# First four row tiles turned as centred rows, their loads on two queues, and a new order of the work

## The chip, the cores and the metric

The kernel runs on one core of a Trainium2 chip. A core has five engines with their own instruction streams: TensorE (PE) for matmuls and transposes through a matmul, VectorE (DVE), ScalarE (ACT), GpSimd (POOL) and SyncE (SP). TensorE writes only to PSUM, in banks; the other engines copy results from there to SBUF. Transfers between HBM and SBUF, and transposes during a transfer, are issued by an engine's queue (here SP, POOL and, in few places, ACT) and carried out by 16 DMA engines.

The metric is the device time of one execution in microseconds, as the median of several runs. A profiled execution gives in addition a trace of every instruction and transfer. Its span runs from the first to the last instruction; the time of the same execution is a little longer than its span.

## The reference

With x of 2048 rows and 512 columns (bf16), LN a layernorm over a row without weights, and xn = LN(x), the result is `x + s * g`:

- **s**: q, k, v = xn @ wqkv, in 32 heads of 16 columns. Row t attends to the eight rows t, t-2, ..., t-14 (rows below 0 are masked), with a softmax over the eight logits; the weighted sum of v is multiplied by wo.
- **g**: `silu(B(xn))`. Within B, `h = gelu(LN(xn) @ w1)`; the four column groups of h are shifted by -1, +1, -2 and +2 rows and multiplied by w2; that is added to xn and gives x1; then `x1 + gelu(LN(x1) @ w3) @ w4`, with 1376 hidden columns.

A layernorm of xn is again a scaling of the centred row: with variance var of a row of x, LN(LN(x)) is (x - mean) times 1/sqrt(var * (1 + eps) + eps * eps).

## The kernel before

The 2048 rows are handled as 16 tiles i of 128 rows, four to a chunk c of 512 rows. Tile i of a chunk holds every fourth row of it, so that a partition reads whole stretches of x. Each operation is a small function ("step") with tile numbers and, for matmuls, the PSUM bank as arguments. One long string, `ORDER`, lists all steps in the order in which they are issued; `ev.2` is the step `ev` for tile 2 and `qk.0.3.2` is q/k column block 3 of chunk 0 into bank 2. The string was made by a planner outside of the kernel. Each engine and each queue works through its own steps in that order, and semaphores hold a step until its operands and its buffer are ready. So a step that waits holds up all that stands behind it on the same engine or queue.

The steps that this case turns on, with their lines:

- `ldxp`, `ldxc` load x by pairs of tiles or by chunks; `ldv`, `ldw1`, `ldqk` (L227 to L241) load the halves of the weights. All go through SP's queue.
- `warmup` (L318) runs matmuls on zeros before there is data.
- `st` (L332) computes mean and variance of a tile on VectorE; `sq0` (L337) the square root of the variance on ScalarE, for tiles 0 to 3; `nm0` (L343) the reciprocal and the normalised tile xr, on VectorE.
- `tr0` (L353) turns a normalised tile of the first chunk on TensorE; `ev0h` and `ev0a` (L359, L363) copy it from PSUM into `xnT`, on ScalarE, in halves or whole.
- From chunk 1 on, `nmv` (VectorE) or `nm` (ScalarE) normalises a tile, and `xT` (L422) turns two tiles with a DMA transpose on SP's queue.
- `v`, `w1` and `qk` (L467, L492, L440) are four matmuls each of 128 x 128 by 512. `v` and `w1` need one turned tile, `qk` all four of its chunk.
- `ev` (L479) copies v out of PSUM and `sv` stores it to HBM; `eh` (L504) applies the gelu to w1's result with a row factor; `eqk` copies q and k.
- `rp`, `rs`, `rr` (L371, L384, L391) compute the row factors: a sum on VectorE, a power on GpSimd, products on VectorE. For tiles 0 to 3, `rr` multiplies the factor by the square root of `sq0`, since the tile that goes into `w1` is normalised already.
- Later come `pw` (products q * k, VectorE), `lg` (their sums over a head, TensorE), the softmax, `vp` (products with v, VectorE) and `ws` (their sum, TensorE), `w2`, `w3`, `w4` and `wo` with `xa`, `ya` and `sg`, which take their results from PSUM on VectorE, and the stores.

In `ORDER` before, the start on TensorE is: warm-up, `tr0` of tiles 0 and 1, `v.0`, `v.1`, `w1.0`, `tr0.2`, `w1.1`, `tr0.3`, then `v` and `w1` of the rest and the eight `qk` of chunk 0.

Of the kernel before, what the change touches and what calls it, by code (L numbers as in the profile page):

```python
# [8 lines left out]
AF = mybir.ActivationFunctionType  # L9
ALU = mybir.AluOpType  # L10
# [12 lines left out]
qk.0.4.1 qk.0.5.5 nmv.6 nmv.7 st.11 ldxc.s.3 st.10 st.8 eqk.0.3 eqk.0.5 qk.0.2.2 eqk.0.0  # L23
qk.0.6.4 eqk.0.2 st.9 eqk.0.4 qk.0.7.3 eqk.0.6 eqk.0.7 pw.0.1 rp.5 st.15 st.13 rp.4 xT.3 hTr.0
ldw2.s hTr.1 w1.4.1 v.5.4 ldwo.s.0 ev.5 w1.5.3 v.4.2 ev.4 qk.1.4.4 rs.4 sv.4 v.6.5 w1.7.2 rr.3
rr.2 eh.4 pw.0.2 kh.1 ev.6 sv.5 rs.5 nb.4 pw.0.0 st.12 eqk.1.4 eh.5 w1.6.1 qk.1.1.4 qk.1.2.3
v.7.5 hTr.2 nm.8 nm.9 w2.1.0 pw.0.3 nb.5 rp.6 eh.6 xT.4 vl.s.1.1 eh.7 st.14 rp.7 lg.0.0 rs.7
eqk.1.2 lg.0.1 ev.7 pw.0.5 w2.0.5 rs.6 eqk.1.1 nm.11 nm.10 pw.0.4 sv.7 qk.1.5.4 sv.6 xT.5
# [45 lines left out]
def kernel(  # L74
# [131 lines left out]
    qs = {"s": nc.sync, "a": nc.scalar, "g": nc.gpsimd}  # L206

    @step
    def ldxc(q, c):
        x_c[c] = rot("xc", c, 2, [P, TPC, D])  # L210
        qs[q].dma_start(
            out=x_c[c],
            in_=x2[c * CH : (c + 1) * CH, :].rearrange("(p i) d -> p i d", i=TPC),
        )
# [69 lines left out]
        nc.gpsimd.memset(mhalf[:], -0.5)  # L284

    @step
    def c_zero():
        nc.gpsimd.dma_start(out=v_dram[0:PADK, :], in_=warm[0:PADK, :])
        nc.gpsimd.memset(hT[:, :, :, 0:HALO], 0.0)
        nc.gpsimd.memset(hT[:, :, :, HALO + S // TPC :], 0.0)  # L290

# [47 lines left out]
            ve1[:, i // 2, i % 2 : i % 2 + 1], mv1[:, i, 1:2], AF.Sqrt, bias=eps_t[:]  # L339
        )  # L340

    @step
    def nm0(i):  # L343
        nc.vector.reciprocal(out=rstd1(i), in_=ve1[:, i // 2, i % 2 : i % 2 + 1])
        nc.vector.tensor_scalar(
            out=xr[i], in0=xtile(i), scalar1=mv1[:, i, 0:1], scalar2=rstd1(i),
            op0=ALU.subtract, op1=ALU.mult,
        )

    tr_t = {}  # L350

    @step
    def tr0(i, b):  # L353
        tr_t[i] = bank(b, (P, ND, P), BF16)
        for dt in range(ND):
            nc.tensor.transpose(tr_t[i][:, dt, :], xr[i][:, dt * P : (dt + 1) * P], ident[:])

    @step
    def ev0a(i):  # L359
        nc.scalar.activation(xnT_tile(0)[:, i, :, :], tr_t.pop(i), AF.Copy)  # L360

    @step
    def ev0h(i, h):  # L363
        nc.scalar.activation(
            xnT_tile(0)[:, i, 2 * h : 2 * h + 2, :], tr_t[i][:, 2 * h : 2 * h + 2, :], AF.Copy
        )
        if h:
            del tr_t[i]
# [121 lines left out]

    @step
    def w1(i, b):  # L492
        c, jj = i // TPC, i % TPC
        pt = mm["w1", i] = bank(b)
        for dt in range(ND):
            nc.tensor.matmul(  # L496
                pt, lhsT=xnT[c][:, jj, dt, :], rhs=w1_sb[:, dt, :],
                start=(dt == 0), stop=(dt == ND - 1),
            )

# [374 lines left out]
```

## Time and profile before

| | us |
|---|---|
| median of 3 runs (189.77 to 190.12) | 189.9 |
| the profiled execution | 190.75 |
| its span | 189.0 |
| PE busy | 182.8 (97%) |
| VectorE busy | 165.1 (87%) |
| ScalarE busy | 112.8 (60%) |
| GpSimd busy | 42.7 (23%) |
| mean DMA rate over the span | 208 GB/s |

The profile is one execution. Busy times are sums over instructions; those of matmuls include the time in which one runs behind another, so PE's is rather too high. "Idle before" an instruction is put down to whatever released it last. The chain of waits follows the work back from the last instruction, at each step to what it waited for. In a tile's answer, "DMA to landing" is the time from issue until the last of the 16 DMA engines has reported. In the windows, each engine has its busy share of the stretch, and the last columns are the granted TensorE clock, the DMA share and GB/s.

### The profile page before, as it was taken

What the parts mean: (1) busy time and instruction counts of PE and PEld (TensorE: products, weight loads), DVE (VectorE), ACT (ScalarE), POOL (GpSimd) and SP (SyncE); (2) the same over time, 40 slices, a digit from 0 to 9 for tenths busy, and PEclk for the clock granted to TensorE, in tenths of its full rate; (3) what the DMA queues carried; (4) which work ended last, traced back from release to release, by engine and by line L of the source; (5) the groups of instructions that cost most, each with busy time, mean ns of one, the idle gap of its engine ahead of it and who ended that gap; (6) DMA issues with size and microseconds to landing.
All of it is one profiled execution on the core that took longest, in us unless ns stands there. A gap on an engine that the chain in (4) does not pass through costs nothing.

```text
span 189.0 us, 3685 instructions
## 1 busy us (share of the span) xinstructions
PE 182.8 (97%) x1430; PEld 87.0 (46%) x1430; DVE 165.1 (87%) x270; ACT 112.8 (60%) x189; POOL 42.7 (23%) x70
## 2 busy tenths in 40 slices
PE   7999999999999999999999999999999999999990
PEld 2444445445444545444444555444455444444450
DVE  2694797997999899999989998999999999989554
ACT  3578669666595636045941465969529664742780
POOL 4157156423010702010450000000050003005350
PEclk9999999999999999999999999999999999999998
DMA  5994986987969929965989929999974999796783
GB/s 164 315 352 115 199 248 141 194 238 137 233 120 286 278 64 224 222 87 190 399 162 361 274 57 134 254 401 277 189 190 95 254 335 238 210 254 106 88 106 116
DMA packets 47842, 39.25 MB, mean 208 GB/s; under 512 B 35251, under 2 KB 41889, under 8 KB 47777
## 3 DMA queue, kind: packets, MB, share of 16 engines
q1 hardware_dynamic: 45008, 35.14, 74.6%
q0 software_dynamic: 2528, 3.69, 10.9%
q8 instruction: 11, 0.18, 0.4%
q10 hardware_dynamic: 288, 0.20, 0.3%
q14 instruction: 7, 0.05, 0.1%
HBM read 26.41 MB, written 5.78 MB: 170 GB/s over the span
## 4 chain that ended last, share of the span: by engine, by line
PE 85%; DMA 4%; DVE 4%; issue 2%; POOL 2%; SPq 1%; ACT 1%; POOLq 0%
PE mm L668 20%; PE mm L685 18%; PE mm L443 15%; PE mm L611 8%; PE mm L496 7%; PE mm L471 6%; PE lg L543 4%; PE mm L768 4%; DMA xc<-in_A_x_dram 3%; PE mm L729 3%; POOL out_dram L835 2%; DMA out_dram<-xr 1%; DVE st L333 1%; DVE xr L775 1%; DVE xr L786 1%
## 5 line engine op out<-in xcount | busy, mean ns | idle before, releaser
L530 DVE TENSOR_TENSOR pw<-qT,kT 128x2048 bf16<-128x2048 bf16 x32 | 38.3, 1214 | 3.4 <-PE lg L543 2.4
L668 PE MATMUL mm<-x1T,w_sb 128*128 128x512 bf16 (+1 forms) x176 | 40.9, 379 | 0.0
L685 PE MATMUL mm<-w_sb,h 128*128 128x512 bf16 (+1 forms) x176 | 39.4, 379 | 0.0
L677 ACT ACTIVATE h<-mm 128x512 bf16<-128x512 f32 (+1 forms) x44 | 23.9, 602 | 23.3 <-PE mm L668 17.6
L716 DVE TENSOR_TENSOR vs<-vs,att 128x4096 bf16<-128x4096 bf16 x16 | 36.2, 2285 | 0.0
L443 PE MATMUL mm<-xnT,wqk_sb 128*128 128x512 bf16 x128 | 30.6, 379 | 0.0
L835 POOL DMA_DIRECT2D out_dram<-xr x12 | 11.0, 1117 | 74.0 <-DVE xr L775 74.0
L668 PEld LDWEIGHTS <-w_sb 128*128 128x128 bf16 (+1 forms) x176 | 17.6, 100 | 20.4
L685 PEld LDWEIGHTS <-h 128*128 128x128 bf16 (+1 forms) x176 | 16.9, 98 | 20.8 <-issue 0.4
L443 PEld LDWEIGHTS <-wqk_sb 128*128 128x128 bf16 x128 | 12.4, 98 | 15.0
L452 ACT ACTIVATE kT<-mm 128x512 bf16<-128x512 f32 x16 | 9.4, 601 | 12.1 <-PE mm L443 11.9
L489 POOL DMA_DIRECT2D v_dram<-vt x16 | 9.6, 601 | 30.6 <-ACT vt L481 27.2
L471 PE MATMUL mm<-w2v_sb,xnT 128*128 128x512 bf16 x64 | 15.8, 379 | 0.0
L496 PE MATMUL mm<-w_sb,xnT 128*128 128x512 bf16 x64 | 15.8, 379 | 0.0
L611 PE MATMUL mm<-w2v_sb,hT 128*128 128x512 bf16 x64 | 15.7, 380 | 0.0
L768 PE MATMUL mm<-wo_sb,oT 128*128 128x512 bf16 x60 | 14.3, 379 | 0.0
L333 DVE BATCH_NORM_STATS2 st<-xc 128x6 f32<-128x512 bf16 x16 | 10.8, 676 | 3.9 <-DMA xc<-in_A_x_dram 3.9
L452 ACT ACTIVATE qT<-mm 128x512 bf16<-128x512 f32 x16 | 9.4, 605 | 7.8 <-PE mm L443 7.7
L635 POOL TENSOR_TENSOR rstd<-nmr,mhalf 128x2 f32<-128x2 f32 x8 | 9.1, 1136 | 19.8 <-DVE nmr L628 19.7
L507 ACT ACTIVATE ht<-mm,rs 128x512 bf16<-128x512 f32 x16 | 10.6, 690 | 4.4 <-PE mm L496 2.3
L696 ACT ACTIVATE xr<-xr 128x512 bf16<-128x512 bf16 x16 | 9.6, 630 | 6.0 <-DVE xr L692 6.0
L692 DVE TENSOR_TENSOR xr<-mm,xr 128x512 bf16<-128x512 f32 x16 | 10.6, 683 | 1.1 <-PE mm L685 0.9
(79 smaller groups left out, 218.5 us busy)
## 6 DMA issues: line engine op xcount, KB each, us to landing
vs<-v_dram SPq DMA_DIRECT2D x32, 512.0 KB, 5.8
v_dram<-vt POOLq DMA_DIRECT2D x16, 128.0 KB, 3.8
out_dram<-in_A_x_dram SPq DMA_DIRECT2D x3, 512.0 KB, 6.5
out_dram<-xr POOLq DMA_DIRECT2D x12, 128.0 KB, 3.5
w_sb<-in_B_w_dram SPq DMA_DIRECT2D x2, 688.0 KB, 4.9
w_sb<-in_B_w_dram SPq DMA_DIRECT2D x2, 640.0 KB, 6.8
xc<-in_A_x_dram SPq DMA_DIRECT2D x4, 256.0 KB, 5.9
wqk_sb<-in_A_wqkv_dram SPq DMA_DIRECT2D x2, 512.0 KB, 7.8
```

What stands on the lines that cost most here:

```text
L443: nc.tensor.matmul(pt, lhsT=wqk_sb[:, dt, nt * P : (nt + 1) * P], rhs=xnT[c][:, :, dt, :], start=(dt == 0), stop=(dt == ND - 1),)
L452: nc.scalar.activation(dst.rearrange("p (n i) -> p n i", i=TPC), mm.pop(("qk", c, nt)).rearrange("p (i n) -> p n i", i=TPC), AF.Copy,)
L471: nc.tensor.matmul(pt, lhsT=xnT[c][:, jj, dt, :], rhs=wv_sb[:, dt, :], start=(dt == 0), stop=(dt == ND - 1),)
L496: nc.tensor.matmul(pt, lhsT=xnT[c][:, jj, dt, :], rhs=w1_sb[:, dt, :], start=(dt == 0), stop=(dt == ND - 1),)
L530: nc.vector.tensor_tensor(out=pw_t[c, u], in0=q_t[c], in1=k_t[c][:, :, DIL * u : DIL * u + CH], op=ALU.mult)
L611: nc.tensor.matmul(pt, lhsT=hT[:, plane, g, p0 : p0 + P], rhs=w2_sb[:, g, :], start=(g == 0), stop=(g == ND - 1),)
L668: nc.tensor.matmul(pt[:fs, :], lhsT=w3_sb[:, dt, ft * P : ft * P + fs], rhs=x1T[c][:, :, dt, :], start=(dt == 0), stop=(dt == ND - 1),)
L677: nc.scalar.activation(h3[c, ft][:fs, :], mm.pop(("w3", c, ft))[:fs, :], AF.Gelu_apprx_tanh)
L685: nc.tensor.matmul(pt, lhsT=h3[c, ft][:fs, jj * P : (jj + 1) * P], rhs=w4_sb[:fs, ft, :], start=(ft == 0), stop=(ft == NF - 1),)
L716: nc.vector.tensor_tensor(out=vv, in0=vv, in1=att[c][:, :, H * jj : H * jj + H].unsqueeze(2).to_broadcast([P, NB * 2, DH, H]), op=ALU.mult,)
L768: nc.tensor.matmul(pt, lhsT=oT[i // 2][:, i % 2, dt, :], rhs=wo_sb[:, dt, :], start=(dt == 0), stop=(dt == ND - 1),)
L835: nc.gpsimd.dma_start(out=rows(out2, i), in_=xr[i], accum_op=ALU.add)
```

## The change

For tiles 0 to 3, VectorE now first writes the centred tile (x minus its mean) into `cen` (step `cn`); `tr0` turns this one, and the copy goes to a buffer `cenT`. `v` and `w1` of these tiles read `cenT`. Their row factors are applied at the copies out of PSUM: `ev` scales by the reciprocal of the square root, and `eh` by the factor of `rs` without the product of `rr`, so `rr.0` and `rr.1` fall away. `rc` is the reciprocal alone. The normalised tiles, which `qk` and later steps need, are made by `nmv.0` to `nmv.3` and turned by two more DMA transposes, `xT.0` and `xT.1`. `cen` and `cenT` share the buffers of the first two `pw` products.

The first loads are split over two queues: x tiles 0 and 1 come in two transfers of one tile each (`ldx`), and the second halves of wv and w1 and the zero rows of the v store are issued by ScalarE. The order on SP is then x0, x1, first half of wv, first half of w1, x2/x3, x4/x5, first half of wqk, x6/x7, `xT.0`, `xT.1`, second half of wqk. The warm-up has 8 wide and 5 narrow matmuls instead of 10 and 8. `ORDER` is a new list throughout; on TensorE it now begins: warm-up, `tr0.0`, `tr0.1`, short warm-up, `v.0`, `v.1`, `tr0.2`, `w1.0`, `w1.1`, `w1.2`, `tr0.3`, `v.2`, `v.3`, `w1.3`, then `qk`. Apart from the steps named here both lists hold the same steps.

```diff
 ORDER = """
-ldxp.s.0 c_warm c_small warmup.10.512.0 sqw c_ident kh.0 ldv.s.0 ldv.s.1 ldxp.s.1 ldw1.s.0
-ldw1.s.1 c_zero st.0 ldxp.s.2 ldxp.s.3 st.1 sq0.0 ldqk.s.0 ldqk.s.1 nm0.0 sq0.1 rp.0 nm0.1
-tr0.0.0 warmup.8.128.1 ev0h.0.0 ev0h.0.1 st.2 tr0.1.2 v.0.1 st.3 ev0h.1.0 ev0h.1.1 sq0.2 v.1.2
-ev.0 nm0.2 sq0.3 rp.1 w1.0.0 ev.1 nm0.3 rs.0 sv.0 st.5 tr0.2.1 ldxc.s.2 w1.1.2 ev0a.2 sv.1 rr.0
-st.4 tr0.3.3 rs.1 v.2.1 ev0a.3 st.7 rp.2 rs.2 w1.2.4 ev.2 st.6 eh.0 v.3.3 sv.2 rp.3 rr.1 w1.3.1
-nmv.4 nmv.5 ev.3 qk.0.1.5 xT.2 eh.1 sv.3 qk.0.0.3 rs.3 qk.0.3.2 eh.2 eh.3 eqk.0.1 c_elog
...
+c_warm c_small ldx.s.0 ldx.s.1 ldv.s.0 ldw1.s.0 ldxp.s.1 ldxp.s.2 c_zero.a warmup.8.512.0
+c_ident ldv.a.1 c_elog ldw1.a.1 st.0 sqw ldqk.s.0 ldxp.s.3 cn.0 st.1 cn.1 sq0.1 sq0.0 tr0.0.1
+tr0.1.0 ev0h.0.0 warmup.5.128.2 rc.0 ev0h.0.1 v.0.3 st.2 ev0h.1.0 ev0h.1.1 v.1.1 rc.1 cn.2 st.3
+sq0.2 ev.0 sv.0 rc.2 sq0.3 nmv.0 ev.1 nmv.1 cn.3 xT.0 rc.3 tr0.2.0 w1.0.3 w1.1.2 ev0a.2 w1.2.0
+rp.0 nmv.2 nmv.3 rs.0 st.4 xT.1 tr0.3.1 v.2.4 ev0a.3 rp.1 st.5 rs.1 eh.1 v.3.1 ldqk.s.1 rp.2
+st.7 rs.2 st.6 rp.3 nmv.4 ldxc.s.2 w1.3.5 ev.2 qk.0.2.2 eh.2 sv.2 nmv.5 qk.0.0.4 rs.3 xT.2
...
     @step
+    def ldx(q, i):
+        if 0 not in x_c:
+            x_c[0] = rot("xc", 0, 2, [P, TPC, D])
+        qs[q].dma_start(out=xtile(i), in_=rows(x2, i))
...
-    def c_zero():
-        nc.gpsimd.dma_start(out=v_dram[0:PADK, :], in_=warm[0:PADK, :])
+    def c_zero(q):
+        qs[q].dma_start(out=v_dram[0:PADK, :], in_=warm[0:PADK, :])
...
-    def nm0(i):
+    cen_t = sb.tile([P, TPC, D], BF16, name="cen", tag="pw0")
+    cenT = sb.tile([P, TPC, ND, P], BF16, name="cenT", tag="pw1")
+
+    def turned(i):
+        return cenT[:, i, :, :] if i < TPC else xnT[i // TPC][:, i % TPC, :, :]
+
+    @step
+    def cn(i):
+        nc.vector.tensor_scalar(
+            out=cen_t[:, i, :], in0=xtile(i), scalar1=mv1[:, i, 0:1], scalar2=None,
+            op0=ALU.subtract,
+        )
+
+    @step
+    def rc(i):
         nc.vector.reciprocal(out=rstd1(i), in_=ve1[:, i // 2, i % 2 : i % 2 + 1])
-        nc.vector.tensor_scalar(
-            out=xr[i], in0=xtile(i), scalar1=mv1[:, i, 0:1], scalar2=rstd1(i),
-            op0=ALU.subtract, op1=ALU.mult,
-        )
...
-            nc.tensor.transpose(tr_t[i][:, dt, :], xr[i][:, dt * P : (dt + 1) * P], ident[:])
+            nc.tensor.transpose(tr_t[i][:, dt, :], cen_t[:, i, dt * P : (dt + 1) * P], ident[:])
...
-        nc.scalar.activation(xnT_tile(0)[:, i, :, :], tr_t.pop(i), AF.Copy)
+        nc.scalar.activation(cenT[:, i, :, :], tr_t.pop(i), AF.Copy)
...
-                pt, lhsT=xnT[c][:, jj, dt, :], rhs=wv_sb[:, dt, :],
+                pt, lhsT=turned(i)[:, dt, :], rhs=wv_sb[:, dt, :],
...
             AF.Copy,
+            scale=rstd1(i) if i < TPC else 1.0,
...
-                pt, lhsT=xnT[c][:, jj, dt, :], rhs=w1_sb[:, dt, :],
+                pt, lhsT=turned(i)[:, dt, :], rhs=w1_sb[:, dt, :],
```

More of the change, by code (lines that the diff above doesn't have):

```diff
@@ L23 @@
[L23 to L28, printed above, removed]
@@ new lines @@
+c_ident ldv.a.1 c_elog ldw1.a.1 st.0 sqw ldqk.s.0 ldxp.s.3 cn.0 st.1 cn.1 sq0.1 sq0.0 tr0.0.1
[3 more added lines that the diff above has]
+st.7 rs.2 st.6 rp.3 nmv.4 ldxc.s.2 w1.3.5 ev.2 qk.0.2.2 eh.2 sv.2 nmv.5 qk.0.0.4 rs.3 xT.2
+qk.0.3.0 sv.1 ev.3 eh.0 eqk.0.0 qk.0.1.3 eqk.0.1 eqk.0.3 eh.3 nmv.7 nmv.6 c_sel qk.0.6.4 xT.3
@@ new lines @@
+qk.0.4.1 st.11 st.8 st.9 c_halo ldxc.s.3 qk.0.5.0 eqk.0.4 hTr.0 eqk.0.6 rp.4 eqk.0.2 rs.4 rr.2
+st.10 ldw2.s qk.0.7.5 hTr.1 eqk.0.7 rp.5 eqk.0.5 v.4.4 rs.5 nb.4 rr.3 w1.4.2 v.5.0 ev.4 ev.5
+kh.0 sv.4 nb.5 st.12 st.13 rp.6 st.14 qk.1.3.4 sv.5 qk.1.1.5 nm.9 eqk.1.3 w1.5.0 qk.1.0.4 sv.3
+eh.4 rs.6 qk.1.6.2 w1.7.1 qk.1.2.3 eh.5 nm.8 rr.4 pw.0.0 pw.0.1 pw.0.2 hTr.2 eqk.1.6 nm.10
+w1.6.2 xT.4 w2.1.0 eh.7 eqk.1.2 vl.s.2.1 qk.1.7.3 xa.1 st.15 rp.7 pw.0.3 nb.6 v.6.1 eqk.1.7
+nm.11 eqk.1.1 w2.0.0 eh.6 w2.2.3 qk.1.5.5 ldwo.s.0 ldw3.s.0 hTr.3 xa.0 nm.12 eqk.1.0 rs.7 v.7.0
@@ new lines @@
+st3s.1 ev.6 xT.5 sv.6 nb.7 nm.15 ev.7 w2.3.4 v.8.1 st3s.0 xa.2 rq.0 sv.7 w1.8.0 xa.3 kh.1 r3.0
+rr.5 st3s.2 w1.9.4 st3s.3 ev.8 lg.0.0 rr.6 lg.0.1 pw.0.4 qk.1.4.1 eh.8 nm.13 rq.1 nm3.1 w2.4.0
+r3.1 pw.0.5 eqk.1.5 xT.6 v.9.5 sv.8 eh.9 nm.14 rr.7 nm3.0 nm3.3 w1.10.4 v.10.3 pw.0.7 ev.9 hTr.4
+eqk.1.4 v.11.1 ev.10 w2.5.5 xT.7 sv.9 sv.10 pw.0.6 w1.11.3 xa.4 kh.2 nm3.2 st3s.4 x1Tr.1
+qk.2.4.0 eh.10 eh.11 lg.0.2 lg.0.3 ev.11 hTr.5 pw.1.0 pw.1.2 w2.7.1 xa.7 sv.11 w1.13.3 v.12.4
+ldw3.s.1 x1Tr.0 eh.13 eqk.2.4 w2.6.1 w1.12.0 w1.14.3 eh.12 pw.1.4 pw.1.3 xa.5 st3s.5 rq.2 r3.2
@@ new lines @@
+w1.15.5 hTr.6 smx.0 w2.9.0 eh.15 eh.14 hTr.7 vl.s.1.1 ldw4.s.2 vl.s.2.0 vl.s.1.0 qk.2.5.2 ev.12
+vl.s.3.0 w2.8.3 sv.12 qk.2.6.4 xa.8 st3s.7 qk.2.0.5 eqk.2.6 nm3.5 w3.0.0.3 eqk.2.0 xa.6 qk.2.7.4
+eg.0.0 nm3.4 pw.1.1 ldw4.s.1 x1Tr.2 eqk.2.5 w3.0.7.1 st3s.6 qk.2.3.2 xa.9 w2.11.3 eqk.2.3 rq.3
+st3s.9 r3.3 ex.0 w2.10.0 xa.11 v.13.2 nm3.6 nm3.7 st3s.8 w3.0.4.3 x1Tr.3 xa.10 lg.1.1 ev.13
+eqk.2.7 lg.1.0 eg.0.7 w3.0.1.4 v.14.0 qk.2.1.1 w3.0.3.2 eqk.2.1 eg.0.4 qk.2.2.5 ev.14 v.15.3
+sv.14 w3.0.6.0 w2.14.1 st3s.11 sms.0 smn.0 pw.1.6 tE.0 pw.1.7 rq.4 r3.4 pw.1.5 eg.0.3 eqk.2.2
@@ L831, in pre, with preh @@
         )
+    @step
+    def preh(q):
+        i = NT - TPC
+        qs[q].dma_start(out=rows(out2, i), in_=rows(x2, i))
     @step
```

79 lines of the change are left out of this document (32 added, 47 removed).

## The prediction

> **What bounds the kernel now.** Read first the busy shares, then TensorE's waits, then the chain of waits, and last the DMA load of the first microseconds.
>
> ```profile
> PE 182.8 (97%) x1430; PEld 87.0 (46%) x1430; DVE 165.1 (87%) x270; ACT 112.8 (60%) x189; POOL 42.7 (23%) x70
> ...
> L356 PE MATMUL mm<-ident,xr 128*128 128x128 bf16 x16 | 1.8, 242 | 0.5 <-DVE xr L345 0.5
> ```
>
> TensorE is busy for 97% of the span, and its only wait behind a producer after the warm-up is 0.5 us in the first transposes. So the list before keeps TensorE fed from about 10 us to the tail; the useful matmuls are the same in both kernels, and a microsecond won or lost ahead of the first q/k matmul stays won or lost.
>
> ```profile
> 2.15 5.68 DMA xc<-in_A_x_dram
> ...
> 7.85 0.71 DVE st L333
> ...
> 8.76 0.59 DVE st L333
> ...
> 9.64 0.42 DVE xr L345
> ...
> 10.11 0.40 PE mm L356 x4
> 10.51 0.94 PE mm L496 x4
> ...
> 15.13 6.91 PE mm L443 x32
> ```
>
> This is the chain in order of time (start, length). It hangs on one transfer: x tiles 2 and 3, issued at 2.15 and landed at 7.83 (call the landing X). Two statistics, one normalisation, the transposes of tile 2 at 10.11; from there TensorE runs without a hole, and the timeline has the first q/k matmul at 14.96.
>
> ```profile
> 2.00:3.00 1.00, 1.00 (x4) 0.44 (x3) 0.00 (x0) 0.21 (x2) 0.82 (x3) 1.00 0.79 296
> ...
> 4.00:5.00 1.00, 1.00 (x4) 0.30 (x2) 0.97 (x3) 0.30 (x1) 0.00 (x0) 1.00 0.78 275
> 5.00:6.00 1.00, 0.76 (x4) 0.13 (x3) 0.89 (x7) 0.29 (x1) 0.02 (x1) 1.00 0.74 241
> ...
> 9.00:10.00 1.00, 0.86 (x4) 0.20 (x2) 0.93 (x5) 0.99 (x4) 0.11 (x1) 1.00 1.06 383
> ```
>
> Windows of 1 us; the last two columns are DMA share and GB/s. The queues move 240 to 300 GB/s from 2 to 7 us and 380 later: the loads are the scarce thing at the start.
>
> ```profile
> L241 SPq DMA_DIRECT2D w_sb<-in_B_w_dram x2: 434/452/469, 2.7 to 3.1; - x2
> ...
> DMA to landing us min/median/max: 5.8/5.9/6.0
> ...
> xnT<-xr SPq DMA_TRANSPOSE x6, 4.2
> ```
>
> The second half of w1, issued at 3.14, lands 6.0 us later, at about 9.2. By then x0 to x3, wv and w1 are in: 1.5 MB.
>
> **The change, part by part.** *Start, tiles 0 and 1.* x0 comes alone (128 KB instead of 256 KB); half of the 1.2 us from the first packet to the landing at 3.6 is saved for it, so its statistics start near 3.1. cn needs no square root. But the list puts both square roots ahead of the first copy out of PSUM, and they wait for tile 1's statistics: 3.1 + 0.94 (statistics) + 0.41 (cn.0) - 0.05 + 0.91 = 5.3, two square roots 0.5, copies from 5.8, first v matmul 0.54 later (6.52 to 7.06 in the timeline before) = 6.3; the warm-ups in between make it 6.6. v.0 and v.1 take 1.73 and end near 8.4 (before 8.83). Two fewer wide warm-ups (0.43 each) and three fewer narrow ones cost nothing: TensorE waits there. The three DMA issues on ScalarE (0.4 each, as its issues at the tail: 0.37) and the table load behind them (1.28) end near 4.0; their cover is the wait until 5.3. If this cover went, each 0.1 would move v, which has slack until X + 1.45, next.
>
> *Tile 2.* From X: 0.73 statistics, 0.18 aggregate, 0.05, 0.41 cn.2, 0.08 with the issues = transposes at X + 1.45. Before it was X + 2.28, as the statistics of tile 3, the square root and the reciprocal lay between: 0.83 gained. But before, w1.0 ran ahead of these transposes (8.83 to 9.69), and now it stands behind them: 0.86 given back. Work from there to the first q/k: two transposes 0.44, three w1 and three v-or-w1 tiles, 6 x 0.863 = 5.18, so X + 7.07; before it was 10.11 + 4.85 = 14.96, or X + 7.13. With X unchanged this is even (0.06).
>
> *The waits that are new there.* w1.0 writes the bank of v.0, so it waits for ev.0, which stands on ScalarE behind sq0.2 (ready at X + 0.95): X + 1.8, 0.1 late. ev.1 stands behind sq0.3 (tile 3's statistics, X + 2.25), ev0a.2 behind it ends at X + 3.6: w1.2 0.1 late; ev0a.3 is ready 0.1 late for v.3: X + 7.4. The q/k bank waits for eh.1, behind a table load of 1.28: X + 7.55.
>
> *The transfer of the normalised tiles.* The first q/k needs xT.0 and xT.1. On VectorE behind X: cn.2 done X + 1.37, tile 3's statistics to X + 2.25, then nmv.0, nmv.1, cn.3, nmv.2, nmv.3 at 0.37 to 0.41 and small ones: X + 4.3. xT.0 goes out near X + 3.0 and holds the queue 1.32; xT.1 follows at X + 4.35. From issue to landing the nearest row in time, xT.2 before (15.17 to 18.79), took 3.6; the range of this stage's rows is 2.9 (hTr.2) to 4.6 (hTr.1). So xT.1 lands at X + 7.25 to X + 8.95; I take 3.5, X + 7.85, as few loads are left in flight by then. This is the last of the three conditions: **first q/k at X + 7.85**, against 14.96. The difference is X - 7.11.
>
> *X itself, the disputed price.* SP's queue now has x0, x1, half of wv, half of w1 and then x2/x3: 1.0 MB up to there, as before. But the other halves (0.5 MB) come on ScalarE's queue from about 2.5 us on and are moved by the same engines, so about 1.5 MB go by before x2/x3 is in. Upper bound: the row with the same bytes, 9.2. Lower bound: both queues together run at the later 380 GB/s from 3 us on: 3.0 + (1.57 - 0.32 MB)/380 GB/s + 0.3 to land = 6.6. The middle is 7.9; I take 8.4, nearer to the row that moved these bytes, because it also held back its last engine (x2/x3 itself: median 5.95, last 7.83). Difference: 8.4 - 7.11 = **+1.3 us**.
>
> The Trainium skill (DMA: Bandwidth & Descriptors, Issuing engines are not separate DMA queues) says that DMAs from several issuers run on the same 16 engines and interleave, and that a second issuer saves only the issue time. By that rule alone X would be the 9.2 of equal bytes, +2.1 us, and the second queue would bring nothing; the idle fifth of the DMA share before 7 us is the room in which the trace could contradict it.
>
> *Costed at nothing.* The second half of wqk now stands behind xT.1 on SP: issued X + 5.7, 4.1 for 512 KB, X + 9.8; wanted after four q/k tiles at X + 11.3, cover 1.5. xT.2 goes out near X + 8.8 and lands by X + 12.4 to X + 13.4; wanted at X + 14.75. VectorE gets four cn (1.65) and loses two rr (0.3): +1.3, which falls into its idle time before the first products (2.4 for GpSimd and 1.0 for ScalarE before).
>
> *The rest of the list.* Running sums of the two lists (matmul steps at 0.863, VectorE steps at their rows) give, at each place where TensorE needs VectorE, the room. The tightest before: 2.5 (pw.3.7 to lg.3.3) and 2.6 (vp.15 to ws.12), where the trace shows 0.4 to 0.55 us of true slack. After: 1.9 (pw.3.7), 2.0 (vp.0 to ws.0), 2.1 (vp.15). But VectorE's own lag behind TensorE, set by the accumulations it must wait for, falls from 2.85 to 2.17. So I take 0, range -0.1 to +0.5. The tail's steps are the same: 0.
>
> Sum: +1.3 on the profiled execution (190.75, of which 189.0 span) = 192.05. The median of the runs is 189.9, 0.85 lower; on it the forecast is **191.2 us**.
>
> **Rivals.**
> (a) *Faster: the two queues fill the idle fifth.* If X falls below 6.75, the first q/k comes before 14.6. At X = 6.6 it is limited by v.1's end: 8.4 + 6.1 = 14.5 for TensorE, 14.45 for xT.1: -0.5, 189.4. If xT.1 also takes 2.9, about -0.9. For it: DMA share 0.74 to 0.83 up to 7 us, c_zero leaves the GpSimd queue. Against: the bytes.
> (b) *No difference (within 0.38 us, which is 0.2% and about what a measurement of this kernel can tell):* X from 6.75 to 7.5. 189.9.
> (c) *Far slower:* X = 9.2, or xT.1 among the loads takes 4.6 (first q/k X + 8.95, which is +2.4 at X = 8.4). 192.0 to 192.6.
> (d) *The new list starves TensorE late*, at ws.0 or lg.3.3: +0.2 to +0.5 on top, 190.3 with an even start. For it: room 0.5 to 0.6 less than before; against: VectorE's smaller lag.
> (e) *The full TensorE clock comes later,* because the warm-up is shorter: the warm-up matmuls took 0.427 each and the v matmuls 0.216, so v.0 and v.1 at the slow rate end 1.7 later, at 10.1, against X + 1.45 = 9.85: +0.3, and it takes rival (a) away.
>
> **Chances.** Forecast (X 7.5 to 9.0, with (d) and (e) in it) 0.52; (c) 0.14; (b) 0.15; (a) 0.19. Faster 0.19, same 0.15, slower 0.66. The range leaves a tenth at each end: 189.4 is (a) at X = 6.6, 192.6 is (c). The forecast's own range is 190.3 to 191.9.
>
> **What would show it.** Tile xc: landing of x2/x3 at 8.4 (7.5 or less refutes the step). Transposes of tile 2 1.45 behind it. The chain: a piece "DMA xnT<-xr" ahead of the first q/k, xT.1 landing 3.5 after its issue; TensorE idle twice before the first q/k, about 1.4 (ahead of tile 2's transposes) and 0.8 in small pieces with 0.3 for xT.1. First q/k at 16.25. After that no TensorE wait; one on VectorE near lg.3.3 or ws.0 would be (d). It is wrong if the loads run at 380 GB/s before 6 us, or if transposes land 2.9 after issue.

## The result and the profile after

| | before | after |
|---|---|---|
| median of 5 runs each, us | 189.9 (189.77 to 190.12) | 192.15 (191.6 to 193.06) |
| ratio, 95% interval | | 1.012 (1.0091 to 1.0148) |
| profiled execution, us | 190.75 | 193.06 |
| its span, us | 189.0 | 191.1 |
| spans of the other executions, us | | 189.6 to 190.3 |
| time outside the span, us | 1.72 to 1.84 | 1.95 to 2.06 |

The change costs 2.25 us, 1.2%. The forecast was 191.2, the range 189.4 to 192.6. About 0.2 of the difference lies outside the span; the rest is in it.

The busy shares of the changed kernel, from its page:

```profile
PE 181.2 (95%) x1410; PEld 86.2 (45%) x1425; DVE 166.1 (87%) x272; ACT 114.3 (60%) x190; POOL 40.6 (21%) x69
```

TensorE does no more than before. Of its 1425 matmuls this trace holds only 1410, so its 95% is too low; all variants of the changed kernel with 1425 recorded matmuls show 96%. What is left of the fall from 97% are new holes. TensorE's waits name them (engine, line, who was waited for: us in total, times, longest):

```profile
PE mm L376 <- DVE cen L361: 2.2, 2, 1.7
PE mm L331 <- DVE warm L282: 1.2, 1, 1.2
PE mm L463 <- ACT ht L526: 0.6, 1, 0.6
PE mm L490 <- ACT cenT L384: 0.2, 1, 0.2
PE mm L463 <- DMA xnT<-xr: 0.2, 1, 0.2
```

Before, the only wait on a producer behind the warm-up was 0.5 us in the first transposes. Now tile 2's transposes wait 1.7 for the centred tile, the first q/k waits 0.2 for the DMA transpose `xT.1`, and a later q/k of chunk 1 waits 0.6 for a gelu. The chain of waits in order of time (start, length) shows how these hang together:

```profile
2.64 6.14 DMA xc<-in_A_x_dram
...
8.80 0.71 DVE st L343
...
10.97 0.63 DVE xr L430 x2
...
12.01 0.64 DVE xr L430 x2
...
13.09 3.20 DMA xnT<-xr
...
16.42 3.63 PE mm L463 x16
20.07 1.08 ACT qT L472 x2
21.16 0.43 ACT ht L526
21.59 7.69 DMA hT<-ht
...
29.36 0.70 ACT ht L526
...
30.10 1.02 PE mm L463 x4
```

Read it from the top. x2/x3 lands at 8.78 (7.83 before). VectorE then makes the statistics and the centred tiles of tiles 2 and 3 and, partly in between, all four normalised ones; `xT.1` goes out at 13.09 and lands 3.2 later, and the first q/k starts at 16.42 (14.96 before): 1.46 later. From there the delay doesn't only persist, it grows. The first transpose of the gelu's results, `hTr.0`, takes 7.7 us (4.0 before). A gelu of chunk 1 needs that buffer back, and the q/k behind it needs the gelu's bank. ScalarE's row in the timeline shows the wait (start, length, work, idle time before it):

```profile
29.36 1.26 ACT L526 ACTIVATE ht<-mm,rs 128x512 bf16<-128x512 f32 x2 [1.41 <-DMA hT<-ht]
```

The starts of two q/k matmuls are 0.94 apart there, in place of the usual 0.22, so TensorE loses 0.73. After it TensorE has no wait of the kind that the rival with the late list spoke of. The last matmul starts at 186.26, before at 184.28: 1.98 later, which is 1.46 + 0.73 less 0.2 won back on the way.

The windows of 1 us (busy shares by engine, then granted clock, DMA share, GB/s) show what the loads make of the DMA engines:

```profile
2.00:3.00 1.00, 1.00 (x4) 0.41 (x3) 0.00 (x0) 0.02 (x1) 0.75 (x4) 1.00 0.83 239
...
5.00:6.00 1.00, 0.48 (x8) 0.27 (x6) 0.77 (x4) 0.68 (x4) 0.00 (x0) 1.00 1.08 374
...
9.00:10.00 1.00, 0.00 (x0) 0.00 (x0) 0.96 (x4) 0.25 (x2) 0.00 (x0) 1.00 0.98 335
```

From 5 to 6 us the rate is 374 GB/s, before it was 241. But from 2 to 5 us it is lower than before: 239, 193 and 265 against 296, 261 and 275. Up to 9 us 2.2 MB were moved, against 2.1 before and 2.2 in a second trace of the kernel before, which follows below. So the two queues use the engines better only after 5 us, and the bytes put ahead of x2/x3 cost more than that. The last window shows TensorE wholly idle.

One more window belongs to the 7.7 us of `hTr.0`. Chunk 3's load (issued at 21.01, landed at 27.50) and `hTr.0` were both under way when it came:

```profile
26.00:27.00 1.00, 1.00 (x7) 0.41 (x6) 0.00 (x0) 0.83 (x2) 0.20 (x1) 1.00 0.04 4
```

The engines moved 4 GB/s there. So it isn't only bytes ahead of it that `hTr.0` waited for. In the second trace of before, the poorest full window while `hTr.0` was under way (20.73 to 24.41) is this:

```profile
22.00:23.00 1.00, 1.00 (x7) 0.46 (x5) 1.00 (x2) 0.04 (x1) 0.00 (x0) 1.00 1.61 160
```

### The profile page after: what moved, and what is told of

Read it like the earlier page. It is cut to its first block, busy times and chain, and to the rows that moved or that the text cites. A ratio compares the mean times of both kernels' runs of the same rounds, so it can differ in the third digit from the quotient of the medians.

```text
span 191.1 us, 3664 instructions
## 1 busy us (share of the span) xinstructions
PE 181.2 (95%) x1410; PEld 86.2 (45%) x1425; DVE 166.1 (87%) x272; ACT 114.3 (60%) x190; POOL 40.6 (21%) x69
## 4 chain that ended last, share of the span: by engine, by line
PE 82%; DMA 9%; DVE 4%; ACT 2%; SPq 1%; issue 1%; DVEq 0%; ACTq 0%
PE mm L687 20%; PE mm L704 20%; PE mm L463 12%; PE mm L630 7%; PE mm L787 6%; PE mm L515 5%; PE mm L490 4%; PE lg L562 4%; DMA hT<-ht 4%; PE mm L748 4%; DMA xc<-in_A_x_dram 3%; DMA xnT<-xr 2%; DVE st L343 1%; DVE xr L430 1%; ACT ht L526 1%
## 5 line engine op out<-in xcount | busy, mean ns | idle before, releaser
L687 PE MATMUL mm<-x1T,w_sb 128*128 128x512 bf16 (+1 forms) x176 | 41.8, 379 | 0.0
L463 PE MATMUL mm<-xnT,wqk_sb 128*128 128x512 bf16 x128 | 31.1, 379 | 0.8 <-ACT ht L526 0.6
L696 ACT ACTIVATE h<-mm 128x512 bf16<-128x512 f32 (+1 forms) x44 | 24.4, 600 | 9.0 <-PE mm L687 8.9
L762 ACT ACTIVATE o<-mm 128x512 bf16<-128x512 f32 x16 | 9.0, 596 | 13.8 <-PE mm L748 13.8
L654 POOL TENSOR_TENSOR rstd<-nmr,mhalf 128x2 f32<-128x2 f32 x8 | 7.6, 944 | 41.7 <-DVE nmr L647 26.5
L630 PE MATMUL mm<-w2v_sb,hT 128*128 128x512 bf16 x60 | 15.2, 379 | 0.2
L490 PE MATMUL mm<-w2v_sb,xnT 128*128 128x512 bf16 x47 | 12.1, 379 | 0.1
```

The lines of the kernel that those rows point to most:

```text
L463: nc.tensor.matmul(pt, lhsT=wqk_sb[:, dt, nt * P : (nt + 1) * P], rhs=xnT[c][:, :, dt, :], start=(dt == 0), stop=(dt == ND - 1),)
L490: nc.tensor.matmul(pt, lhsT=turned(i)[:, dt, :], rhs=wv_sb[:, dt, :], start=(dt == 0), stop=(dt == ND - 1),)
L630: nc.tensor.matmul(pt, lhsT=hT[:, plane, g, p0 : p0 + P], rhs=w2_sb[:, g, :], start=(g == 0), stop=(g == ND - 1),)
L687: nc.tensor.matmul(pt[:fs, :], lhsT=w3_sb[:, dt, ft * P : ft * P + fs], rhs=x1T[c][:, :, dt, :], start=(dt == 0), stop=(dt == ND - 1),)
L696: nc.scalar.activation(h3[c, ft][:fs, :], mm.pop(("w3", c, ft))[:fs, :], AF.Gelu_apprx_tanh)
```

## The experiments

A landing is always that of the last of the 16 DMA engines; the median engine stands beside it where the two differ much. This table has the milestones of all traces (us from the span's start) and the medians; each ratio is to runs of the kernel before that were made beside that variant (medians 189.86 to 190.01):

| kernel | x2/x3 landed (median engine) | first q/k | median of runs | ratio to before, 95% interval |
|---|---|---|---|---|
| before | 7.83 (5.95) | 14.96 | 189.9 | |
| before, again | 6.76 (5.67) | 14.07 | 189.91 | 1.0009 (0.9994 to 1.0023) |
| after | 8.78 (7.67) | 16.42 | 192.15 | 1.012 (1.0091 to 1.0148) |
| x2/x3 ahead | 7.59 (6.36) | 15.18 | 190.7 | 1.0039 (1.0026 to 1.0053) |
| one queue | 8.11 (6.34) | 15.73 | 191.59 | 1.0087 (1.0072 to 1.0103) |
| chunk 3's load ahead | 8.73 (7.36) | 16.28 | 192.73 | 1.0155 (1.0115 to 1.0194) |
| before on two queues | 7.62 (7.34) | 14.75 | 190.51 | 1.0031 (1.0019 to 1.0042) |
| zero rows on GpSimd | 7.75 (7.58) | 16.20 | 191.66 | 1.0092 (1.0076 to 1.0109) |
| centred rows alone | 6.27 (5.58) | 15.29 | 191.01 | 1.0052 (1.0035 to 1.0069) |
| x2/x3 ahead, wqk early | 7.49 (6.16) | 15.40 | 190.92 | 1.0044 (1.003 to 1.0058) |
| centred, no `xT.0`/`xT.1` | 5.93 (5.58) | 13.73 | 190.35 | 1.0016 (1.0001 to 1.0032) |
| x0 and x1 apart | 7.64 (5.93) | 14.77 | 190.27 | 1.0014 (0.9998 to 1.0029) |
| two tiles centred | 6.04 (5.42) | 14.30 | 190.07 | 0.9998 (0.9987 to 1.0009) |
| after, no `xT.0`/`xT.1` | 9.67 (7.62) | 17.21 | 191.86 | 1.0082 (1.0062 to 1.0102) |

### The landing of x2/x3

**x2/x3 ahead of the first half of w1**, on SP's queue; nothing else differs from the changed kernel.

```
-c_warm c_small ldx.s.0 ldx.s.1 ldv.s.0 ldw1.s.0 ldxp.s.1 ldxp.s.2 ...
+c_warm c_small ldx.s.0 ldx.s.1 ldv.s.0 ldxp.s.1 ldw1.s.0 ldxp.s.2 ...
```

> The changed kernel with one swap on SP's queue: x2/x3 goes ahead of the first half of w1. Theory 1 (the start is late because bytes stand ahead of x2/x3, and the first q/k follows its landing X by 7.64 us): 0.26 MB less ahead, at some 350 GB/s 0.7 earlier, X = 8.05, transposes of tile 2 at 9.45, first q/k at 15.7 instead of 16.42, time 0.7 us under the changed kernel's 192.15. Rival (X is set by one late DMA engine, whatever stands ahead): X stays at 8.6 to 8.9, time within 0.2 of 192.15. Theory 2 (a stall of 0.73 near 30 us comes from the transposed h of tiles 0 and 1 being late) expects that stall here too.

It gains 1.45 us on the changed kernel, twice what was expected. The start of its chain:

```profile
2.13 5.46 DMA xc<-in_A_x_dram
...
9.48 2.75 PE mm L515 x12
...
14.40 0.70 ACT ht L526
...
15.18 7.07 PE mm L463 x32
```

x2/x3 lands 1.19 earlier (7.59) and the first q/k comes 1.24 earlier: the landing carries through one to one. The first q/k is at X + 7.59, now behind the gelu whose bank it takes over, with `xT.1`, which landed at 15.05, hardly earlier. `hTr.0` still took 6.4 us, but the hole near 30 us is gone; why is not shown. So the position of one 256 KB load behind another accounts for 1.45 of 2.25 us.

**All loads on SP's queue**, x2/x3 behind the whole of wv:

```
-c_warm c_small ldx.s.0 ldx.s.1 ldv.s.0 ldw1.s.0 ldxp.s.1 ldxp.s.2 c_zero.a ...
-c_ident ldv.a.1 c_elog ldw1.a.1 st.0 ...
+c_warm c_small ldx.s.0 ldx.s.1 ldv.s.0 ldv.s.1 ldxp.s.1 ldw1.s.0 ldw1.s.1 ldxp.s.2 c_zero.a
+... c_ident c_elog st.0 ...
```

> The changed kernel with the weight halves back on SP's queue in the order before (x0, x1, wv, wv, x2/x3, w1, w1). Theory 1: 1.0 MB ahead of x2/x3 as in the kernel before, X = 7.8, first q/k at 15.45, time 1.0 under the changed kernel: 191.1. Rival (the second queue is a gain in itself and without it the DMA engines are idle for longer): X no earlier than 8.6, time 192 or more.

It gains 0.56, half of what was expected. With fewer bytes ahead of x2/x3 the median engine is in at 6.34 against 7.67; the last engine came 1.8 later than that, and the kernel waits for the last. A wait of 0.2 on the gelu near 30 us stays.

**The kernel before with the second halves of wv and w1 on ScalarE's queue**:

```
-ldxp.s.0 c_warm c_small ... ldv.s.0 ldv.s.1 ldxp.s.1 ldw1.s.0
-ldw1.s.1 c_zero st.0 ...
+ldxp.s.0 c_warm c_small ... ldv.s.0 ldv.a.1 ldw1.s.0 ldxp.s.1
+ldw1.a.1 c_zero st.0 ...
```

> The kernel before with one part of the change alone: second halves of wv and w1 issued by ScalarE, and the first half of w1 ahead of x2/x3 on SP. Theory 1: X goes from 7.83 to about 8.7, the transposes of tile 2 follow at X + 2.28 = 11.0 instead of 10.11, and all of it stays to the end: 0.9 over the 189.9 of before. Rival (the second queue is harmless or helps): X no later than 7.9, time 189.9 or less.

It costs 0.55 by itself. Two chains show where. This is its own:

```profile
0.73 3.21 DMA xc<-in_A_x_dram
...
9.92 0.39 PE mm L356 x4
...
14.91 6.91 PE mm L443 x32
```

And this is the chain of the kernel before, run again:

```profile
0.73 2.77 DMA xc<-in_A_x_dram
...
9.47 0.22 PE mm L356 x4
...
14.24 6.91 PE mm L443 x32
```

The very first load, x0/x1, lands at 3.94 in place of 3.49, although nothing stands ahead of it on its queue: the transfers that ScalarE issues at 0.86 and 1.34 share the engines with it. (In the changed kernel ScalarE issues them later, at 1.82 and 2.46, and x0 and x1 are in at 3.15 and 3.77.) Then x2/x3 lands at 7.62 with its engines nearly together (median 7.34), and the first q/k comes 0.68 later than in the second trace of before.

**The zero rows back on GpSimd**, in the changed kernel (`c_zero.a` becomes `c_zero.g`):

> The changed kernel with the zero rows of the v store issued by GpSimd, as before, instead of ScalarE. Two things are in question. Outside of the span the changed kernel and the three experiments on it take 1.95 to 2.04 us, the kernel before and the one with the weights on two queues 1.73 to 1.85: if the zero rows on ScalarE's queue make this, it falls to 1.8 here, time 0.2 lower; if not, 2.0. And the last engine for x2/x3 lags by 1.1 to 1.9 us behind the median in all of the changed kernel's forms, not in the one with the weights alone on two queues: if the zero rows cause it, x2/x3 lands by 7.9 and the time falls by 0.7 more; if not, 8.5 to 8.9.

It gains 0.5. Without the zero rows ScalarE's loads go out at 0.74 and 1.25; x1 then lands at 4.87 (3.77 in the changed kernel) and x2/x3 at 7.75, with its engines together, as the theory had it. The time outside the span stays at 2.06 to 2.13. TensorE's timeline has a surprise behind that:

```profile
7.39 3.09 PE L490 MATMUL mm<-w2v_sb,cenT 128*128 128x512 bf16 x8
```

These eight matmuls took 1.89 in the changed kernel. The full clock was granted only at 9.80 here, so v.0 and v.1 ran at half rate, and tile 2's transposes came at 10.31 = X + 2.56 in place of X + 1.38. This is what rival (e) of the prediction priced, but not its cause: the changed kernel has the same shorter warm-up and got the full clock at 5.30. It uses up what the earlier landing won, at the first q/k all but 0.2.

### The transfers between 15 and 30 us

**Chunk 3's load ahead of `xT.3`**, as in the list before, in the changed kernel:

```
-... nmv.7 nmv.6 c_sel qk.0.6.4 xT.3 qk.0.4.1 st.11 st.8 st.9 c_halo ldxc.s.3 qk.0.5.0 ... hTr.0
+... nmv.7 nmv.6 c_sel qk.0.6.4 ldxc.s.3 xT.3 qk.0.4.1 st.11 st.8 st.9 c_halo qk.0.5.0 ... hTr.0
```

> The changed kernel with one swap: the load of the last x chunk goes out ahead of the second transpose of chunk 1 (as in the kernel before), not behind it. The start stays (first q/k near 16.4). Theory 2 (the load stood in front of the transpose of h of tiles 0 and 1 and made it 7.7 us long, against 4.0 before; gelu of tile 4 waited for its buffer, and a q/k matmul for that): this transpose lands 1 to 3 us earlier, the stall of 0.73 near 30 us is gone, time 0.7 under 192.15. Rival (the DMA engines have a backlog there, and the order doesn't matter): the transpose of h lands at 28.5 or later, the stall stays over 0.5, time within 0.2 of 192.15.

No gain. The gelu's wait is gone, and another takes its place, as the chain shows:

```profile
19.98 6.36 DMA xnT<-xr
...
26.38 1.90 PE mm L463 x8
```

`hTr.0` lands 5.9 us after its issue in place of 7.7, but now `xT.3` stands behind the 512 KB load and takes 6.4 (3.2 in the changed kernel), and chunk 1's first q/k waits 0.4 for it. The median engine had `xT.3` in at 24.72, the last one at 26.34, and from 25 to 26 us the engines moved 11 GB/s. The theory that the order of this load is the cause falls.

**The second half of wqk ahead of `xT.0`**, on top of x2/x3 ahead:

```
-c_ident ldv.a.1 c_elog ldw1.a.1 st.0 sqw ldqk.s.0 ldxp.s.3 cn.0 ... eh.1 v.3.1 ldqk.s.1 rp.2
+c_ident ldv.a.1 c_elog ldw1.a.1 st.0 sqw ldqk.s.0 ldxp.s.3 ldqk.s.1 cn.0 ... eh.1 v.3.1 rp.2
```

> The swap of the first experiment (x2/x3 ahead of the first half of w1) and the second half of wqk loaded ahead of the two transposes, not behind them. Theory 2b (0.5 MB of wqk and two more transposes between 11 and 20 us leave a backlog of transfers, in which the transposes of h and of chunk 1 take 6 to 8 us instead of 4): the transpose of h of tiles 0 and 1 takes 4 to 5 us instead of 6.3, no wait of TensorE after the first q/k in any execution, time 0.2 to 0.5 under the 190.7 of that experiment and a spread under 0.6. Rival (backlog from another source): transposes still over 6 us and time within 0.2 of 190.7. A cost that may come with it: xT.0 and xT.1 behind 0.5 MB more, first q/k up to 0.3 later.

190.92 against 190.7: no gain either. The load no longer stands between the transposes, but `xT.1` now shares the engines with it: it lands at 15.26 and the first q/k waits 0.5 for it. `hTr.0` still takes 7.3 (15 of the 16 engines are done after 5.8) and `hTr.1` 8.2.

### The parts alone

**The kernel before, again**, unchanged:

> The kernel before, unchanged, for a second trace. The traced execution of before has a span of 189.0, while sixteen other executions have 187.9 to 188.5. Theory (its start was held by x2/x3 landing at 7.83, 1.9 us after the median of the 16 engines; in most executions no engine lags so): x2/x3 lands before 7.3, the transposes of tile 2 follow w1.0 at once, the first q/k starts at 14.2 to 14.5 instead of 14.96, span 188.0 to 188.5. Rival (the difference lies elsewhere): first q/k within 0.1 of 14.96 and TensorE waits later on shorter, or the part outside of the span differs.

The median repeats (189.91). The trace is another: first q/k at 14.07, not 14.96, and a span of 188.1, not 189.0. So the profiled execution on which the prediction's sum stands was a high one, because one DMA engine brought x2/x3 1.9 after the median engine.

**Centred rows in the list before**, with all loads as before, and `xT.0`, `xT.1` added:

```
-ldw1.s.1 c_zero st.0 ldxp.s.2 ... nm0.0 sq0.1 rp.0 nm0.1
+ldw1.s.1 c_zero.g c_halo st.0 cn.0 ldxp.s.2 ldxp.s.3 st.1 cn.1 sq0.0 sq0.1 rc.0 rc.1 ldqk.s.0
...
+ev0h.1.0 ev0h.1.1 sq0.2 rc.2 nmv.0 nmv.1 xT.0 v.1.2 ev.0 sq0.3 rc.3 nmv.2 nmv.3 xT.1 rp.1 w1.0.0
```

> The kernel before with the turning of centred tiles alone: its loads, its queue order and its list, with the new steps put where their operands are ready, and the two transposes of the normalised tiles. My step (with the same landing X nothing is won, since the first q/k hangs on xT.1): first q/k no earlier than before, at 14.4 to 15.2, and the backlog of transfers that follows is smaller than in the changed kernel as the second half of wqk is loaded early: time 189.8 to 190.6. Rival (centring is the gain, and the loads take it away): first q/k at 13.9 or earlier and time under 189.5.

It is 1.15 slower than before, beyond the expected range. A wait of TensorE says why:

```profile
PE mm L463 <- DMA xnT<-xr: 1.2, 1, 1.2
```

In its chain of waits the same place reads:

```profile
10.96 4.19 DMA xnT<-xr
...
15.29 7.07 PE mm L463 x32
```

x2/x3 is in at 6.27, v and w1 of the four tiles are through at 13.9, and TensorE then stands 1.22 us for `xT.1`. Issued at 10.96, while wqk was still on its way (it landed at 12.05), it takes 4.2 us; in the changed kernel, with that half of wqk behind it, 3.2. `xT.0` took 4.8.

**The same without `xT.0` and `xT.1`**; the left-out work is told in the expectation:

```
-                pt, lhsT=wqk_sb[:, dt, nt * P : (nt + 1) * P], rhs=xnT[c][:, :, dt, :],
+                pt, lhsT=wqk_sb[:, dt, nt * P : (nt + 1) * P], rhs=(cenT if c == 0 else xnT[c])[:, :, dt, :],
```

> The experiment with the centred turning alone, without its two DMA transposes: q and k of chunk 0 are taken from the centred tiles too, so the row factor of q and k is left out for the first 512 rows. Theory 3 (the price of the centred turning is that q/k must wait for xT.1, which is issued behind the last normalisation and travels 3 to 5 us; 1.22 us of TensorE's time in the trace): first q/k at 13.9, no wait after it, time 1.2 under the 191.0 of that experiment, 189.7 to 189.9. Rival (the wait is only where another delay shows, or the added work on VectorE costs it): time over 190.4.

0.66 faster than with the transposes, about half of what the wait of 1.2 had promised, and still 0.35 over before. In its trace everything is as hoped: first q/k at 13.73 and a span of 187.8, the shortest of all traces. But that execution was the fastest of twelve (189.58 to 191.07), and where the others lost their time no trace shows. The part of the transposes is shown, the remaining 0.35 stays open.

**Only tiles 0 and 1 centred**, `xT.0` ahead of wqk's second half, tiles 2 and 3 turned normalised as before:

```
+        return cenT[:, i, :, :] if i < 2 else xnT[i // TPC][:, i % TPC, :, :]
+            src = cen_t[:, i, :] if i < 2 else xr[i]
+            scale=rstd1(i) if i < 2 else 1.0,
```

> A version that could beat both: the loads and the list before, centred turning for tiles 0 and 1 alone (their normalised tiles go by one DMA transpose, xT.0, issued near 7 us ahead of the second half of wqk), tiles 2 and 3 turned normalised as before. By theory 3 xT.0 lands by 12.5, ahead of the first q/k, so that nothing waits; v.0 comes at 6.3 instead of 6.7, and the first q/k at 13.7 to 13.9 if x2/x3 lands by 6.5, else at X + 7.13. Time 189.5 to 189.8. Rival (the added transpose and 0.8 us on VectorE ahead of tile 2 cost as much as they save): 189.9 to 190.4.

The same as before (ratio 0.9998), as the rival had it. `xT.0` took 4.6 us, from 6.84 to 11.48, and no one waited for it; no wait remains but the warm-up's. The first q/k is at 14.30 and not by 13.9, although x2/x3 landed at 6.04: v.0 came at 6.91 and not at 6.3, with the full clock granted only at 6.31.

**x0 and x1 in two loads** in the kernel before (`ldxp.s.0` becomes `ldx.s.0 ldx.s.1`):

> The kernel before with one part of the change alone: x tiles 0 and 1 in two loads of 128 KB instead of one of 256 KB. The statistics of tile 0 start at 3.15 instead of 3.5, those of tile 1 at 4.0, so v.0 comes at most 0.35 earlier; tile 2 (X + 2.28 = 9.0) then limits. Expected 189.6 to 189.9, 0 to 0.3 under the kernel before. Rival (the small loads cost more than they bring, each a DMA more on the queue): 190.0 to 190.4. The part outside of the span: 1.77 unless the two small loads make the 2.0 of the changed kernel.

Not faster, and in the rival's range: x0 lands at 3.15 in place of 3.49, but the trace's x2/x3 lands at 7.64 with a median engine at 5.93, and the first q/k is at 14.77. The 0.3 won at x0 isn't seen in the median.

**The changed kernel without `xT.0` and `xT.1`**, edited as above:

> The changed kernel without xT.0 and xT.1: q and k of chunk 0 are taken from the centred tiles (their row factor is left out for the first 512 rows), and the second half of wqk is no longer held behind them. In the trace of the changed kernel TensorE was ready for q/k at 16.05 and began at 16.42, so the start by itself gains only 0.2 to 0.4 (X + 7.4 instead of X + 7.64): the landing of x2/x3 sets it there. Theory 2b (the two transposes and the late half of wqk make the backlog that stalls TensorE near 30 us): this stall of 0.73 is gone too, time 190.9 to 191.4. Rival (the rest is the landing of x2/x3 and the new list): 191.7 or more.

191.86, at the rival's end. The medians of the spans are 190.1 here and 190.2 in the changed kernel: in this setting the two transposes cost the span next to nothing, and the 0.3 of difference is nearly all outside it (1.73 to 1.82 here). Two waits of its trace tell what sets it instead:

```profile
PE mm L490 <- DMA w2v_sb<-in_A_wqkv_dram: 1.0, 1, 1.0
...
PE mm L463 <- ACT ht L526: 0.5, 1, 0.5
```

The loads landed late (x2/x3 9.67, wv's half 7.45; median engines 7.62 and 4.62), and the wait for `hTr.0` is there again, 7.5 us after its issue, although neither extra transpose nor a late half of wqk stood ahead of it. So the late transposes before 30 us don't come from the two new ones. They follow the new list: in all seven traces with it, 17 to 21 packets (the pieces of a transfer) of 256 bytes took 1.25 to 2.8 us each between 23 and 29 us (the median of such packets is 0.02), and in six of them the engines moved at most 24 GB/s in one window of 1 us there; in the seven with the list of before, no such packet took over 1.2 before 34 us. That holds on one queue and on two, with the two transposes and without. What in the list does it was not found. One difference that stands beside it in all fourteen traces is the step `c_halo`, which zeroes the edge columns of `hT` on GpSimd: with the new list it runs at 18.7 to 21.2 us, shortly ahead of `hTr.0`, while the kernel before has this work in `c_zero`, at 2.2 us, and the other variants of its list have it there too. Whether it bears on the late transposes was not tried. This trace is of the slowest of six executions (193.15), partly for a reason that the last section tells.

## Why the prediction was right, and where not

The direction, the place and the mechanism at the start were right; the size was short by 0.95 us, and the time is just outside of the forecast's own range (190.3 to 191.9). It lies where case (c) put it, 192.0 to 192.6, but neither of (c)'s conditions held, so that match is luck. The two first traces differ by 2.31 us where 1.3 was forecast. Of the missing 1.0, 0.17 lie at the first q/k, 0.52 between it and the last matmul (the stall of 0.73, less what was won back), 0.12 behind that and 0.21 outside the span.

- *Start, tiles 0 and 1.* v.0 forecast at 6.6, measured 6.61; v.1's end forecast near 8.4, measured 8.4. The shorter warm-up cost nothing in this trace, with full clock from 5.30.
- *Tile 2.* Transposes forecast at X + 1.45, measured X + 1.38.
- *The waits that are new there.* The q/k bank behind the gelu was put at X + 7.55; x2/x3 ahead, where this wait decides, has X + 7.59.
- *The transfer of the normalised tiles.* Issue of `xT.1` forecast X + 4.35, measured X + 4.31; issue to landing 3.5, measured 3.2. First q/k forecast X + 7.85, measured X + 7.64. Case (c)'s price for `xT.1` among the loads, X + 8.95, is close to what centred rows alone showed, X + 9.02, but there it was issued later (X + 4.69) and took 4.2, not 4.6. The sum's range for such a transfer, 2.9 to 4.6, left out a row of the same trace: `xT.3` took 5.6 (18.89 to 24.49).
- *X itself.* Forecast 8.4, measured 8.78, within the bounds 6.6 to 9.2. The two errors, +0.38 here and -0.21 behind X, partly cancel: +1.46 at the first q/k where +1.3 was forecast. Moving 256 KB out from ahead of x2/x3 brought it in 1.19 earlier, so their place in the queue is shown as the cause, though 256 KB at the expected 350 GB/s make only 0.7. The sign that would have refuted the step, 380 GB/s before 6 us, was nearly there in one window (374), but the three windows before it were slower than in the kernel before.
- *The Trainium skill's rule* (DMA: Bandwidth & Descriptors, Issuing engines are not separate DMA queues) would have had x2/x3 at the 9.2 of equal bytes. The trace lies nearer to it than to the sum's middle of 7.9: 8.78, with the median engine at 7.67. One queue, with 0.5 MB less ahead, landed x2/x3 at 8.11, earlier than two.
- *Costed at nothing*: this step failed. It took the 4.1 us of the second half of wqk and the landings of `xT.2` one by one, and each was in time (`xT.2` landed at 21.6). It did not ask when the transfers behind them would land. `hTr.0` took 7.7 us in place of 4.0, and TensorE lost 0.73. Why it was late stays open: neither the order of chunk 3's load nor the second half of wqk nor the two new transposes is the cause by itself, as their experiments show. What the traces show is that packets of 256 bytes take over 1.2 us in all seven with the new list, in place of 0.02, and that the engines moved 4 GB/s from 26 to 27 us here.
- *The rest of the list* at 0, -0.1 to +0.5: no wait of TensorE on VectorE appears late, so rival (d) is not seen. But there was no sum for the DMA queue.
- *Not in the sum at all*: 0.2 us outside the span.
- *The base.* The sum was made against an execution in which the start was held 0.9 by a late DMA engine, and took 0.85 off at its end. That this came out is luck: the changed kernel's trace lies 0.91 over its own median (193.06 against 192.15). Against the second trace of before, the first q/k comes 2.35 later, not 1.46. The clean accounts are the medians: spans 188.2 and 190.2, +2.0, and +0.2 outside.

What is shown in the changed kernel itself: the place of x2/x3 in its queue is worth 1.45 of the 2.25 us, and 0.2 lie outside the span. The remaining 0.6 was not isolated; the stall before 30 us, which cost 0.73 in one trace, may be part of it. Put into the kernel before, the loads on two queues cost 0.55 and the centred rows with their DMA transposes 1.15, of which 0.66 are the two transposes. These are not shares of the 2.25: in the changed kernel ScalarE's loads go out about 1 us later, and leaving out the transposes gained only 0.3 there, nearly all outside the span. Rival (a) is refuted: x2/x3 never landed before 7.4 where ScalarE issued loads.

## What to carry to other kernels

Work that is moved from TensorE to a DMA transpose takes its place in a queue that already feeds TensorE: follow the queue's transfers in order up to the next one that somebody waits for, as one follows an engine's instructions, and don't price them by their bytes alone. Here the loads on two queues shared the same engines, and the late one was the load behind them; put the load on which the chain hangs ahead in its queue, and count every byte of both queues in front of it. Before a sum is made against one profiled execution, look whether its first landings are those of the median engine or of one late engine.

## What was not expected of the hardware

- *One late engine.* In some executions one or a few of the 16 DMA engines bring x2/x3 0.6 to 2.05 us after the median engine (before 1.88, one queue 1.77, x0 and x1 apart 1.71, after without transposes 2.05); in others they stay within 0.35 (centred without `xT.0`/`xT.1` 0.35, before on two queues 0.28, zero rows on GpSimd 0.17). In the last two ScalarE's first DMA is a weight's half, issued by 0.86; whether that matters was not tried, and the cause stays open.
- *A second queue can delay the first.* x0/x1 landed at 3.94 in place of 3.49, x1 at 4.87 in place of 3.77, each with nothing new ahead of it on its own queue.
- *Transposes by DMA* took 2.8 to 3.4 us with little else under way (`hTr.2` in the second trace of before, `xT.0` in the changed kernel), 4.2 to 4.8 beside the loads of wqk (centred rows alone), and 3.7 to 9.0 for `xT.3`, `hTr.0` and `hTr.1` behind chunk 3's load.
- *The clock's opening* moved from 3.82 (centred rows alone) to 9.80 us (zero rows on GpSimd). In the changed kernel without its transposes it opened at 4.15 and closed again for 3.41 us. Three windows of its trace show it (TensorE's busy time first, granted clock third from the end):

```profile
4.15:7.57 3.42, 1.53 (x16) 0.86 (x15) 1.65 (x5) 1.89 (x8) 0.00 (x0) 1.00 0.99 347
7.57:10.98 3.41, 3.41 (x8) 0.93 (x7) 1.25 (x5) 0.34 (x2) 0.00 (x0) 0.50 1.08 375
10.98:14.40 3.42, 3.29 (x22) 1.63 (x22) 3.35 (x15) 1.88 (x4) 1.60 (x2) 1.00 0.31 105
```

  TensorE was busy 1.53 of the first 3.42 us, and the next 3.41 ran at half clock. In the changed kernel 1.85 of 3.41 (from 8.71 to 12.12) kept the full clock. So in this execution the late landing of wv seems to have cost both the wait and half the rate behind it. The Trainium skill (TensorE: Matmul & The Clock Gate, What's actually happening) speaks of a free-running window of some 3.4 us after which an idle TensorE is throttled; the trace agrees on the length, 3.41 us, and here a window in which TensorE was 45% busy was followed by half clock, in one execution.
- *Time outside the span.* It is 1.95 to 2.13 us in the changed kernel and the five variants that keep both its x0/x1 split and its two more transposes, and 1.72 to 1.85 in before and all variants that lack one or both (before on two queues and centred rows alone among them). Moving the zero rows off ScalarE did not change it (2.06 to 2.13). Why, was not tried.
